# The norm of segment 2 transposed on TensorE, and a new order of the work

## The chip, the cores and the metric

The kernel runs on one core of one Trainium2 chip. The core has five engines that work side by side, each through its own queue in order: PE (matrix products; its weight loads are listed apart as PEld), DVE (vector), ACT (activation functions), POOL (general) and SP, which here only issues DMA transfers. Their results meet in two memories: SBUF, and PSUM with eight banks, into which PE writes. The metric is the time of one execution on the device in microseconds; the median of several runs counts.

## What is computed

The reference is one transformer block on 2048 tokens of 448 features. A conditioning vector gives six modulation vectors; the block is a modulated norm, an attention with a memory over four segments of 512 tokens, a second modulated norm, and a gated feed-forward part.

```python
mod = (silu(c) @ w_mod).reshape(1, 6, 1, -1)          # sa, ca, ga, sb, cb, gb
h = layernorm(x) * (1 + ca) + sa
x = x + ga * A(h)
h = layernorm(x) * (1 + cb) + sb
x = x + gb * B(h)

def A(x):                      # 16 heads of 28; 4 segments of 512
    q, k, v = split(x @ wq), split(x @ wk), split(x @ wv)
    M, z = 0, 0
    for s in range(4):
        a_dot = softmax(q[s] @ k[s].T * 28**-0.5 + causal_mask) @ v[s]
        a_mem = phi(q[s]) @ M / (phi(q[s]) @ z + 1e-6)
        o[s] = g * a_mem + (1 - g) * a_dot             # g = sigmoid(beta)
        M, z = M + phi(k[s]).T @ v[s], z + sum(phi(k[s]))
    return o @ wo

def B(x):
    return (sigmoid(x @ w_gate) * (x @ w_up)) @ w_down
```

Here phi(t) is t + 1 for positive t and exp(t) otherwise.

## The kernel before

**Stages.** Four segments of 512 tokens, each of four tiles of 128 tokens, pass through the same stages. `ln1` (from L618) normalizes x and brings it into the layout hT, features on partitions. `proj` (L655) makes q, k and v from it: 32 matmuls at L665 for q and k, 16 at L686 for v, with evictions out of PSUM by ACT (L673, L690). `attention` (L730) handles four heads at once, in four such groups (hc): logits at L746 into four adjacent PSUM banks, exp by ACT at L755, the causal mask by POOL at L761, the product with v at L769, and, after segment 0, the product with the memory at L783; DVE turns and scales the result (L776 to L817). `memory` (L703) applies phi to k, transposes it by DMA (pk<-pq, L708) and updates M (L714 to L727). `wo_ln2` (L821) applies the output weights (L831), adds the residual (L835) and makes the second norm. `ffn` (L843) makes 14 chunks of 128 hidden features: gate and up matmuls (L848, L856), tanh by ACT (L882), the gating product by DVE (L885), then the down product (L895), the residual (L901) and the output transfer (L903).

**The norm and its transposition.** `layer_norms` (L557) does statistics on DVE (L566, L567), the reciprocal root on POOL (L573, L574) and the scaling into an xn buffer on DVE (L582). There are six xn buffers. From there two ways lead to hT:

- For segments 0 and 1, `ln1` takes the branch at L622: PE transposes (L634, sixteen 128x128 products with the identity into four PSUM banks), and each bank is evicted with the modulation in the same instruction, two by ACT (L642) and two by DVE (L645).
- For segments 2 and 3, and for the second norm of all segments, SP issues four DMA transposes (`transposed`, L590; they appear as L592, hT<-xn), and four instructions modulate hT in place (`modulated`, L596): two on ACT (L602) and two on DVE (L605).

**The loads.** All weights come in once by DMA, nearly all issued by SP: q, k, v, x, the modulation weights (wm, at L347), the output weights (L505), then gate, up and down (L509 to L512). At most eight transfers are out at a time, and transposes go through the same queue. The output and down weights are multiplied by ga and gb in place (L544 on POOL; L551 on DVE for the first `wdd` of 14 chunks, on POOL for the rest).

**The order.** The order of instructions on every engine is worked out on the host before the program is built. Every piece of work is a node with an engine, a duration in ns, its dependencies, the buffers and banks it takes, and a priority. `Graph.run` (L110) plays the program through with these durations; whenever an engine is free, it takes the ready node with the highest sum of priority and remaining path. A load's duration is its size over a rate in bytes per ns (`load`, L327). The priorities are the numbers in `PRM` (L22), one per kind of work; `attention` is also held back by release times from `pace` (L914), and those of segment 0 get `a0` on top. `Graph.fill` (L187) puts dummy matmuls (L930, L933) into gaps of PE that the plan shows. On the chip each engine then follows its list in order, whatever the real durations are.

```python
    def pace(i):
        return PRM["T0"] + PRM["STEP0"] * min(i, NHC) + PRM["STEP"] * max(i - NHC, 0)
```

Of the kernel before, what the change touches and what calls it, by code (L numbers as in the profile page):

```python
# [11 lines left out]
ALU = mybir.AluOpType  # L12
# [8 lines left out]

PRM = dict(T0=6000, STEP0=500.0, STEP=10100.0, lg=77000, ex=-37000, mask=-11000, wo=58000, tanh=44500,  # L22
           up=77000, f=172500, dn=-486800, phi=-81000, t=-83000, ln1_1=-16000, ln1_2=-57000, ln1_3=-52000,
           mem=-12000, pj_0=44000, pj_1=-15000, pj_2=-94000, pj_3=9000, ot=339000, stall=300, wds=18000,
           wos=144000, wdd=4, mod=35000, a0=39000, w0=-37000, stay=120000)

# [181 lines left out]
def kernel(  # L208
# [16 lines left out]
    nc = tc.nc  # L225
# [118 lines left out]
    def load_wm(engs, j0, nj, flat, prio, deps=()):  # L344
        t = flat[0:CP, 0:NK * nj * D].rearrange("p (k n) -> p k n", k=NK)
        h = NK // len(engs)
        ns = [load(eng, t[:, i * h:(i + 1) * h, :], wm_cols[:, i * h:(i + 1) * h, j0 * D:(j0 + nj) * D],  # L347
                   CP * h * nj * D * 2, prio=prio, deps=deps, rate=240.0 if nj < 4 else 290.0)
              for i, eng in enumerate(engs)]
        for j in range(j0, j0 + nj):  # L350
            wm_at[j] = t[:, :, (j - j0) * D:(j - j0 + 1) * D]
            wml[j] = ns
# [97 lines left out]
    def mod_cols(j, vi, prio):  # L450
        b = bank()

        def mm():

            for kc, r0, r1 in ((0, 0, P), (1, 0, P), (2, 0, P), (3, 0, KR), (3, KR, P))[:4 if vi < 2 else 5]:
                for k in range(NK):
                    nc.tensor.matmul(pf(b)[r0:r1, kc:kc + 1], lhsT=wm_at[j][:, k, kc * P:kc * P + r1 - r0],
                                     rhs=silu[:, k:k + 1], start=(k == 0), stop=(k == NK - 1))
        n = add("PE", (16 if vi < 2 else 20) * 55, mm, [n_silu, *wml[j]], take=[b], prio=prio, mode="F")

# [21 lines left out]
    def padded(st, dst, loads, eng, prio):  # L482
        ns = []
        for k in range(NK):
            def fn(k=k, r=ROWS[k]):
# [3 lines left out]
                else:  # L489
# [15 lines left out]
    l_wo = [load("SP", wo_sb[h * HP:h * HP + Dh, :, :],  # L505
                 A_wo.rearrange("(c h e) n -> h e c n", h=4, e=Dh)[h], Dh * NHC * D * 2, [n_wopad], prio=lp - MEG * 4, rate=225.0)
            for h in range(4)]
# [49 lines left out]
    def layer_norms(srcs, deps, prio=0, hT=None, prev=None, twice=False):  # L557
# [13 lines left out]
        def rstd():  # L571
            r = rs_r[:, mv.at, 0:w]
            nc.gpsimd.tensor_scalar(r, mv_r[:, mv.at, 0:w, 1], EPS, None, op0=ALU.add)  # L573
            nc.gpsimd.tensor_tensor(r, r, mhalf[:, 0:w], ALU.pow)  # L574
        b = pool_op(860 if w == 1 else 1330, rstd, stats, prio, use=[mv])
        got = []
        for t, src in enumerate(srcs):
            xn = Slot("xn")

            def norm(t=t, src=src, xn=xn):  # L580
                for dst, x in ((xn_r[:, xn.at, 0:D], src), (xn_r[:, xn.at, D:NK * P], src[:, 3 * P:D]))[:1 + twice]:
                    nc.vector.tensor_scalar(dst, x, mv_r[:, mv.at, t, 0:1], rs_r[:, mv.at, t:t + 1],  # L582
                                            op0=ALU.subtract, op1=ALU.mult)
            n = dve(300 + 110 * twice, norm, [b, n_pads, prev], prio, take=[xn] if prev or not hT else [xn, hT],
                use=[mv], lock=0)
            prev = n
            got.append((n, xn))
# [30 lines left out]
    def ln1(s):  # L618
        hT = Slot("hT")
        out_ = []  # L620
        tiles = range(s * TPS, (s + 1) * TPS)
        if s < 2:  # L622
            top = BIG - 2 * MEG if s == 0 else PRM["ln1_1"]
            if s == 0:
# [69 lines left out]
    def phi(src, dst, deps, slots, take, prio):  # L694

        e = Slot("e")
        a = act(530, lambda: nc.scalar.activation(e_r[:, e.at, 0, :], src(), AF.Exp), deps, take=[e], use=slots, prio=prio)  # L697
        b = dve(210, lambda: nc.vector.tensor_scalar(e_r[:, e.at, 1, :], src(), 0.0, 1.0, op0=ALU.max, op1=ALU.add),
                [a], use=[e, *slots], prio=prio, lock=0)
# [30 lines left out]
    def attention(s, hc, oT, release, prev):  # L730
# [58 lines left out]
        def rec():  # L789
# [3 lines left out]
            nc.vector.tensor_tensor(r, r, coef[:, 0:w, hc, :], ALU.mult)  # L793
        r = dve(450 if w == 2 else 350, rec, [*parts, n_coef, n_opad], take=[R], use=[A], prio=PRM["t"] + a0, lock=320 if w == 2 else 230)

# [169 lines left out]
```

## Time and profile before

| what | value |
|---|---|
| median of 7 runs | 255.34 us (253.79 to 257.28) |
| the profiled execution | 255.64 us, of which the span is 253.6 us |
| mean granted TensorE clock | 0.991 of full speed |
| busy: PE, DVE, ACT, POOL | 241.5, 182.1, 157.3, 100.8 us |
| sum of all exp instructions (L755, 48) | 77.2 us on ACT |
| transposes by PE (L634, 32) | 2.3 us on PE, 219 ns each |
| evictions with modulation, ACT / DVE (L642 / L645) | 828 and 786 / 542 ns each |
| modulation in place, ACT / DVE (L602 / L605) | 829 and 820 / 516 ns each |
| DMA transposes hT<-xn (24), issue to landing | 2.4 us at least, 4.6 median, 10.9 at most |
| DMA transposes pk<-pq (12), issue to landing | 2.4 us at least, 2.4 median, 6.3 at most |

The span is the time from the first to the last instruction; the rest of an execution lies around it. An engine's busy time is the time in which at least one of its instructions runs. PE's matmuls are pipelined, so that neighbours overlap in the records: a 128x512 matmul is listed with 380 ns, and the next starts 216 ns after it. The page also cuts the span into 40 slices of 6.3 us, with a digit for the busy tenths of each:

```profile
PE   7999976889999999999999999999999999999994
DVE  7589935648977989999976999982487882453223
ACT  2589958989999969988915756866342232323110
PEclk9999997999999999999999999999999999999999
DMA  6999999321241010013401000210100022100002
GB/s 189 301 296 297 307 156 290 77 29 21 23 83 22 3 21 16 9 21 44 84 14 63 0 0 3 54 28 8 49 18 4 0 41 41 39 18 19 0 3 72
```

The input transfers fill the first 45 us (rows DMA and GB/s). PEclk is the TensorE clock that was granted, in tenths.

### The profile page before, as it was taken

To read this page: it belongs to the slowest core of one execution; us is meant where nothing else is said; L and a number is where in the kernel's file an instruction comes from. 1 tells how busy PE (TensorE), PEld (TensorE's weight loads), DVE (VectorE), ACT (ScalarE), POOL (GpSimd) and SP (SyncE) were. 2 spreads that over 40 slices of the span, in tenths; PEclk is the share of its full clock that TensorE was granted. 3 is DMA by queue.
4 is the path that set the end of the run, shared out by engine and by line. 5 is a ranking of instruction groups with operands and counts; after the bars stand their busy time and mean duration, and the time that the engine had idled before them with its cause. 6 is when DMAs were issued, how large, how long until landed. Compare 5 with 4: busy or idle time off the path is not lost.

```text
span 253.6 us, 4521 instructions
## 1 busy us (share of the span) xinstructions
PE 241.5 (95%) x1643; PEld 102.7 (40%) x1643; DVE 182.1 (72%) x411; ACT 157.3 (62%) x202; POOL 100.8 (40%) x164
## 2 busy tenths in 40 slices
PE   7999976889999999999999999999999999999994
PEld 2545432334434344444453433334333445334342
DVE  7589935648977989999976999982487882453223
ACT  2589958989999969988915756866342232323110
POOL 7745932224997544756350246632131220000000
PEclk9999997999999999999999999999999999999999
DMA  6999999321241010013401000210100022100002
GB/s 189 301 296 297 307 156 290 77 29 21 23 83 22 3 21 16 9 21 44 84 14 63 0 0 3 54 28 8 49 18 4 0 41 41 39 18 19 0 3 72
DMA packets 30142, 17.52 MB, mean 69 GB/s; under 512 B 20648, under 2 KB 28776, under 8 KB 30120
## 3 DMA queue, kind: packets, MB, share of 16 engines
q1 hardware_dynamic: 29592, 16.60, 28.5%
q10 hardware_dynamic: 528, 0.63, 0.9%
q8 instruction: 13, 0.21, 0.4%
q14 instruction: 9, 0.07, 0.1%
HBM read 10.67 MB, written 1.84 MB: 49 GB/s over the span
## 4 chain that ended last, share of the span: by engine, by line
PE 65%; DVE 12%; DMA 10%; ACT 6%; POOL 2%; issue 2%; SPq 1%; DVEq 0%; ACTq 0%
PE ps L848 28%; PE ps L895 15%; PE ps L665 5%; DMA pk<-pq 4%; PE ps L856 4%; PE ps L746 3%; DMA hT<-xn 3%; PE ps L831 3%; PE ps L769 3%; ACT pT L755 3%; DMA wd_sb<-in_A_wk_dram 2%; DVE fT L885 2%; PE ps L686 2%; DVE A L776 2%; POOL wo_sb L544 2%
## 5 line engine op out<-in xcount | busy, mean ns | idle before, releaser
L755 ACT ACTIVATE pT<-ps 128x2048 bf16<-128x2048 f32 (+1 forms) x48 | 77.2, 1608 | 16.8 <-PE ps L746 14.1
L761 POOL TENSOR_SCALAR_AFFINE_SELECT pT<-pT 128x512 bf16<-128x512 bf16 x64 | 44.1, 702 | 73.5 <-ACT pT L755 73.5
L882 ACT ACTIVATE tt<-ps 128x512 f32<-128x512 f32 x56 | 33.4, 603 | 51.9 <-PE ps L856 40.3
L885 DVE SCALAR_TENSOR_TENSOR fT<-tt,ps 128x512 bf16<-128x512 f32 x56 | 37.9, 682 | 26.7 <-ACT tt L882 22.7
L848 PE MATMUL ps<-hT,wu_sb 128*128 128x512 bf16 x182 | 48.5, 380 | 0.5 <-ACT pT L755 0.5
L848 PE MATMUL ps<-hT,wg_sb 128*128 128x512 bf16 x182 | 48.7, 381 | 0.0
L895 PE MATMUL ps<-wd_sb,fT 128*128 128x448 bf16 x224 | 45.7, 353 | 0.0
L895 PEld LDWEIGHTS <-fT 128*128 128x128 bf16 x224 | 21.4, 98 | 21.0 <-issue 0.8
L848 PEld LDWEIGHTS <-wu_sb 128*128 128x128 bf16 x182 | 16.9, 98 | 21.3 <-issue 1.8
L848 PEld LDWEIGHTS <-wg_sb 128*128 128x128 bf16 x182 | 15.5, 98 | 24.0 <-issue 9.7
L746 PE MATMUL ps<-qT,kT 28*128 28x512 bf16 (+3 forms) x256 | 17.6, 302 | 3.8 <-ACT pT L755 3.5
L566 DVE BATCH_NORM_STATS2 st<-x_sb 128x6 f32<-128x448 bf16 x32 | 19.5, 610 | 2.4 <-DMA x_sb<-in_A_x_dram 2.2
L776 DVE STREAM_TRANSPOSE A<-ps 128x512 f32<-128x512 f32 x28 | 19.1, 700 | 0.6 <-PE ps L783 0.5
L815 POOL TENSOR_TENSOR O<-U 128x448 bf16<-128x448 f32 x12 | 13.7, 1140 | 11.3 <-DVE U L813 11.3
L582 DVE TENSOR_SCALAR xn<-x_sb,mv,rs 128x448 bf16<-128x448 bf16 (+1 forms) x48 | 16.9, 408 | 0.8 <-POOL rs L574 0.8
L700 DVE TENSOR_TENSOR pq<-e 128x512 bf16<-128x512 bf16 x24 | 12.1, 506 | 7.3 <-ACT e L697 6.0
L665 PE MATMUL ps<-hT,wq_sb 128*128 128x512 bf16 x64 | 16.7, 380 | 0.1
L665 PE MATMUL ps<-hT,wk_sb 128*128 128x512 bf16 x64 | 16.5, 380 | 0.0
L574 POOL TENSOR_TENSOR rs<-rs,mhalf 128x1 f32<-128x1 f32 (+1 forms) x23 | 15.2, 663 | 1.9
L901 DVE TENSOR_TENSOR ot<-ps,x_sb 128x448 bf16<-128x448 f32 x16 | 9.8, 620 | 8.1 <-PE ps L895 7.3
L686 PE MATMUL ps<-wv_sb,hT 128*128 128x448 bf16 x64 | 15.3, 386 | 0.0
L813 DVE TENSOR_TENSOR U<-A,R 128x896 f32<-128x896 f32 x12 | 13.3, 1105 | 1.8 <-POOL O L815 1.6
(104 smaller groups left out, 285.8 us busy)
## 6 DMA issues: line engine op xcount, KB each, us to landing
out_dram<-ot SPq DMA_DIRECT2D x16, 112.0 KB, 1.7
fT<-in_w_mod_dram SPq DMA_DIRECT2D x1, 1568.0 KB, 11.7
x_sb<-in_A_x_dram SPq DMA_DIRECT2D x3, 448.0 KB, 5.4
wg_sb<-in_B_w_gate_dram SPq DMA_DIRECT2D x3, 448.0 KB, 7.6
wu_sb<-in_B_w_up_dram SPq DMA_DIRECT2D x3, 448.0 KB
wd_sb<-in_B_w_down_dram SPq DMA_DIRECT2D x2, 448.0 KB
wd_sb<-in_B_w_down_dram SPq DMA_DIRECT2D x2, 336.0 KB, 6.4
pT<-in_w_mod_dram ACTq DMA_DIRECT2D x1, 392.0 KB
```

The costliest lines, as they stand in the source:

```text
L566: nc.vector.bn_stats(st_r[:, st.at, :], src)
L582: nc.vector.tensor_scalar(dst, x, mv_r[:, mv.at, t, 0:1], rs_r[:, mv.at, t:t + 1], op0=ALU.subtract, op1=ALU.mult)
L665: nc.tensor.matmul(pf(b), lhsT=w_sb[:, kc, hc * 4:(hc + 1) * 4, :].rearrange("p h e -> p (h e)"), rhs=hT_r[:, hT.at, kc, :], start=(kc == ...
L686: nc.tensor.matmul(pf(b)[:, 0:D], lhsT=hT_r[:, hT.at, kc, t * P:(t + 1) * P], rhs=wv_sb[:, kc, :], start=(kc == 0), stop=(kc == NK - 1))
L746: nc.tensor.matmul(ps[:, lg.at + hs, o:o + nq], lhsT=kT_r[r, k.at, hc, kb * P:(kb + 1) * P], rhs=qT_r[r, q.at, hc, kb * P:L], start=True, ...
L755: nc.scalar.activation(pT_r[:, pT.at, :, w0:w0 + wid], ps[:, lg.at:lg.at + 4, 0:wid], AF.Exp, scale=scale)
L761: nc.gpsimd.affine_select(out=blk, in_=blk, compare_op=ALU.is_ge, fill=0.0, base=0, pattern=[[0, 4], [1, P]], channel_multiplier=-1)
L776: nc.vector.transpose(A_r[:, A.at, i, :, :].rearrange("p b e -> p (b e)"), pf(b))
L848: nc.tensor.matmul(pf(b), lhsT=w_sb[:, k, fc * P:(fc + 1) * P], rhs=hT_r[:, hT.at, k, :], start=(k == 0 and not late), stop=(k == n - 1 an ...
L882: a = act(500, lambda gp=gp, tt=tt: nc.scalar.activation(tt_r[:, tt.at, :], pf(gp), AF.Tanh, scale=0.5), [g], use=[gp, tt], prio=PRM["tanh"])
L885: fns.append(dve(605, lambda up=up, tt=tt, ft=ft: nc.vector.scalar_tensor_tensor(fT_r[:, ft.at, :], tt_r[:, tt.at, :], 1.0, pf(up), op0=AL ...
L895: nc.tensor.matmul(pf(b)[:, 0:D], lhsT=fT_r[:, fts[fc].at, t * P:(t + 1) * P], rhs=wd_sb[:, fc, :], start=(fc == 0), stop=(fc == NFC - 1))
```

## The change

Segment 2 takes the branch of segments 0 and 1: sixteen PE transposes and four evictions that modulate, in place of four DMA transposes and four modulations. Segment 3 and the second norms keep the DMA transposes.

The numbers that the planner works with change too: the rates of the modulation and output weight loads are lower, and some durations are set anew. All entries of `PRM` but a few have new values, so that the order on every engine is worked out again. The instructions are otherwise the same, but for two chunks of the down weights (`wdd` 4 to 6) that DVE scales instead of POOL.

```diff
-PRM = dict(T0=6000, STEP0=500.0, STEP=10100.0, lg=77000, ex=-37000, mask=-11000, wo=58000, tanh=44500,
-           up=77000, f=172500, dn=-486800, phi=-81000, t=-83000, ln1_1=-16000, ln1_2=-57000, ln1_3=-52000,
-           mem=-12000, pj_0=44000, pj_1=-15000, pj_2=-94000, pj_3=9000, ot=339000, stall=300, wds=18000,
-           wos=144000, wdd=4, mod=35000, a0=39000, w0=-37000, stay=120000)
+PRM = dict(T0=5000, STEP0=-1500.0, STEP=10000.0, lg=76000, ex=15000, mask=49000, wo=79000, tanh=-15500,
+           up=81000, f=175500, dn=-495800, phi=-82000, t=-80000, ln1_1=-17000, ln1_2=-57000, ln1_3=-52000,
+           mem=-32000, pj_0=36000, pj_1=5000, pj_2=-43000, pj_3=9000, ot=399000, stall=300, wds=-42000,
+           wos=144000, wdd=6, mod=-26000, a0=99000, w0=-36000, stay=120000)
...
-                   CP * h * nj * D * 2, prio=prio, deps=deps, rate=240.0 if nj < 4 else 290.0)
+                   CP * h * nj * D * 2, prio=prio, deps=deps, rate=190.0 if nj < 4 else 245.0)
...
-        n = add("PE", (16 if vi < 2 else 20) * 55, mm, [n_silu, *wml[j]], take=[b], prio=prio, mode="F")
+        n = add("PE", (16 if vi < 2 else 20) * 40, mm, [n_silu, *wml[j]], take=[b], prio=prio, mode="F")
...
-                 A_wo.rearrange("(c h e) n -> h e c n", h=4, e=Dh)[h], Dh * NHC * D * 2, [n_wopad], prio=lp - MEG * 4, rate=225.0)
+                 A_wo.rearrange("(c h e) n -> h e c n", h=4, e=Dh)[h], Dh * NHC * D * 2, [n_wopad], prio=lp - MEG * 4, rate=195.0)
...
-        b = pool_op(860 if w == 1 else 1330, rstd, stats, prio, use=[mv])
+        b = pool_op(860 if w == 1 else 1500, rstd, stats, prio, use=[mv])
...
-            n = dve(300 + 110 * twice, norm, [b, n_pads, prev], prio, take=[xn] if prev or not hT else [xn, hT],
+            n = dve(300 + 210 * twice, norm, [b, n_pads, prev], prio, take=[xn] if prev or not hT else [xn, hT],
...
-        if s < 2:
-            top = BIG - 2 * MEG if s == 0 else PRM["ln1_1"]
+        if s < 3:
+            top = BIG - 2 * MEG if s == 0 else PRM[f"ln1_{s}"]
...
-        b = dve(210, lambda: nc.vector.tensor_scalar(e_r[:, e.at, 1, :], src(), 0.0, 1.0, op0=ALU.max, op1=ALU.add),
+        b = dve(260, lambda: nc.vector.tensor_scalar(e_r[:, e.at, 1, :], src(), 0.0, 1.0, op0=ALU.max, op1=ALU.add),
...
-        r = dve(450 if w == 2 else 350, rec, [*parts, n_coef, n_opad], take=[R], use=[A], prio=PRM["t"] + a0, lock=320 if w == 2 else 230)
+        r = dve(520 if w == 2 else 430, rec, [*parts, n_coef, n_opad], take=[R], use=[A], prio=PRM["t"] + a0, lock=330 if w == 2 else 250)
```

## The prediction

> **What bounds the kernel now.** I read the engine rows first, then the stages, then the waits of the one bad stage, then its instructions in order of time.
>
> The windows view, cut at the places where the character of the work changes (columns: stretch, its length, then busy microseconds of PE, PEld, DVE, ACT, POOL with instruction counts, granted clock, DMA share, GB/s):
>
> ```profile
> 11.00:33.50 22.50, 22.36 (x186) 10.29 (x183) 18.92 (x55) 21.54 (x32) 15.93 (x27) 1.00 1.15 289
> 33.50:40.00 6.50, 3.09 (x29) 1.24 (x29) 2.96 (x8) 3.34 (x5) 0.70 (x1) 1.00 1.02 214
> 40.00:57.00 17.00, 14.81 (x121) 6.33 (x121) 8.35 (x23) 15.08 (x20) 5.03 (x8) 0.90 0.61 110
> 57.00:76.00 19.00, 18.41 (x142) 7.88 (x140) 16.41 (x39) 18.47 (x27) 14.65 (x22) 1.00 0.25 42
> 76.00:137.00 61.00, 60.98 (x454) 26.05 (x442) 54.73 (x116) 47.61 (x56) 31.94 (x43) 1.00 0.15 31
> 137.00:167.00 30.00, 28.97 (x204) 10.95 (x200) 26.97 (x60) 20.41 (x21) 13.64 (x22) 1.00 0.09 18
> 167.00:248.00 81.00, 81.00 (x449) 34.21 (x448) 42.84 (x81) 27.18 (x39) 10.38 (x17) 1.00 0.07 19
> ```
>
> From 76 us to the end PE has work at every moment (0.02 + 1.03 + 0.00 us idle in 172), so the end is the sum of PE's work plus whatever PE lost earlier. From 11 to 76 us the feed-forward stage has not begun and ACT is the full engine: 21.54 of 22.5, 15.08 of 17, 18.47 of 19. In between lies a hole, 33.5 to 40, in which every engine is half empty. The waits view of 33 to 57 us names it (us in total, times, longest):
>
> ```profile
> DVE hT L605 <- DMA hT<-xn: 4.3, 2, 3.4
> PE ps L746 <- ACT pT L755: 3.5, 2, 3.3
> ACT hT L602 <- DMA hT<-xn: 3.2, 1, 3.2
> PEld L714 <- DMA pk<-pq: 2.4, 2, 1.6
> ACT pT L755 <- PE ps L746: 1.9, 2, 1.2
> ```
>
> And the timeline of SP's queue, ACT, DVE and PE there (start, length, what; in brackets the idle time before it and who ended it):
>
> ```profile
> 24.61 10.03 SPq L592 DMA_TRANSPOSE hT<-xn  x4
> 34.69 0.59 SPq L329 DMA_DIRECT2D wu_sb<-in_B_w_up_dram  x1
> 35.38 2.15 SPq L329 DMA_DIRECT2D wd_sb<-in_B_w_down_dram  x4
> 37.63 1.76 SPq L708 DMA_TRANSPOSE pk<-pq  x1
> ...
> 37.39 0.81 ACT L602 ACTIVATE hT<-hT,cols 128x512 bf16<-128x512 bf16 x1 [3.16 <-DMA hT<-xn]
> 38.11 1.86 ACT L755 ACTIVATE pT<-ps 128x2048 bf16<-128x2048 f32 x1
> ...
> 37.43 0.74 DVE L605 TENSOR_SCALAR hT<-hT,cols 128x512 bf16<-128x512 bf16 x2 [3.41 <-DMA hT<-xn]
> ...
> 40.02 0.40 PE L746 MATMUL ps<-qT,kT 28*128 28x384 bf16 x8 [3.33 <-ACT pT L755]
> 40.35 4.13 PE L686 MATMUL ps<-wv_sb,hT 128*128 128x448 bf16 x12
> ```
>
> Segment 2's four transposes sit in SP's queue behind weight loads. SP needs 10.03 us to issue them; the last lands at 37.2. The modulation that waits for them heads ACT's and DVE's in-order queues, so an exp whose logits are long ready starts at 38.11 and the next logits only at 40.02. PE's 3.33 us of silence is then followed by a second loss: the window 40.9 to 44.3 has a granted clock of 0.50, and the 12 matmuls of L686 take 4.13 us where 12 x 189 ns (the spacing of the same matmuls elsewhere) is 2.27.
>
> **The change part by part.** All sums are against the profiled execution: 255.64 us (span 253.6 and 2.0 around it), 0.30 above the median of 255.34.
>
> *A. Four DMA transposes and four modulations of segment 2 go.* The stall they cause is 3.16 us on ACT, 3.41 on DVE, 3.33 on PE. ACT is the full engine around it, so I take ACT's: -3.2. What is late next is the same ACT queue with nothing to wait for; DVE and PE have slack behind it until 57 us.
> Here a rule speaks against the change. In this trace a transpose of this shape costs SP at least 1.19 us and lands 2.4 us after its issue when nothing is ahead of it (median 4.6, worst 10.9). The Trainium skill, "Advanced Engine Details and Errata", section X-Bar Transpose (TRN2), says that transposing DMAs are as fast as plain ones, 350 to 400 GB/s: an estimate from it is 4 x 131 KB / 350 = 1.5 us for the four, so their going would be worth 1.5 and the final sum -2.7. I follow the trace: what is removed is the wait for the last landing with the queue in it, not the transfer.
>
> *B. The half-speed clock after the hole goes with it.* PE loses 4.13 - 2.27 = 1.86 us; the part that ACT felt is the 1.24 us it waited for the late L746. Between 0 and -1.9; I take -1.2.
>
> *C. Sixteen PE transposes come in (L634).* The row for segment 1 is 16 in 1.28 us at 22.54, start to start 56 ns: 16 x 56 = 0.9 us. PE is full in that stage (22.36 of 22.5), so nothing covers it: +0.9. They add a wait, for the four xn of segment 2 from DVE, with projections and logits queued behind them on PE; the last of these xn ended at 25.7 us, and DVE had done their statistics by 19.5, so I charge the wait nothing; DVE's 3.6 idle of 22.5 us there is its cover. The Trainium skill, "TensorE: Matmul & The Clock Gate", Part 4: PE-mode transpose, puts one at about 275 ns in a kernel and says transposes do not count as activity for the clock: by it 16 x 275 = 4.4 us, and the sum would be -0.9. The trace has them overlapping at 219 ns each with the clock at 1.00 from 20 to 30 us; I take 0.9.
>
> *D. Four evictions out of PSUM replace the four modulations.* ACT: 2 x 0.81 us (L642) for 2 x 0.82 (L602), nothing. DVE: 2 x 0.54 (L645) for 2 x 0.41 (L605), +0.3, covered by DVE's idle time (8.65 of 17 us in 40 to 57); if that cover were gone it costs 0.3. Each of the four takes a PSUM bank for about a microsecond, while the logits need four adjacent ones. No row shows that conflict alone; below it is nothing, above it is the longest wait of an exp for logits (L755 on L746), 1.7. I take 0, since segment 1 did the same at 22.5 us and PE idled 0.06 us from 20 to 30.
>
> *E. SP's queue is shorter.* The last up-projection load and the four down-projection loads, issued at 34.69 to 37.5, move ahead by up to the 10.03 us of SP time; the pk transposes behind them landed 6.3 and 4.7 us after issue where 2.4 is normal. PE waited 0.61 and 1.15 us for pk at 45.6 and 52.9. Ends 0 and -1.8; I take the middle, -0.9. Segment 3's four DMA transposes stay, and may come earlier: three of its norms (L582) ran only at 38.08, since the six xn buffers were held until segment 2's transposes had landed.
>
> *F. Everything else is the order.* The planner gets slower load rates (the rates set when matmuls of wm and wo are placed), 40 for 55 ns a matmul of L457, and longer DVE and POOL durations; with them all priorities. What they say: attention of segment 0 is much more urgent (exp -37000 + 39000 becomes 15000 + 99000), heads are released from 5.0 us and the fifth at -1.0 instead of 8.0, one per 10.0 instead of 10.1 us; tanh falls below exp (44500 against -37000 becomes -15500 against 15000); the scaling of the down weights comes later, two more of it on DVE (2 x 0.60 us more there, 2 x 1.10 less on POOL). No row of this trace shows the new order. On the gain side, what is left of PE's losses from 11 to 248 us bounds it: 7.4 idle + 1.9 clock + about 2 of dummy matmuls (L933, 9 x 216 ns) = 11.3, less A, B and E, so -6 at most. On the loss side the nearest row is 137 to 167, where DVE is 90% full and PE loses 1.03 in 30 us; spread over 76 to 248 that is +6. I take 0.
>
> Sum: -3.2 - 1.2 + 0.9 - 0.9 = -4.4. 255.64 - 4.4 = 251.2, and 250.9 against the median.
>
> **The rivals.**
>
> *R1, the hole moves instead of closing.* Segment 3's transposes and the first pk transposes use the same queue and the same loads; the planner still reckons the feed-forward weights at 400 GB/s where the page shows about 300. If the new order puts segment 3's modulation early on ACT and DVE, they wait as segment 2's did. For it: the first of them, issued at 39.5, landed some 5 us later, and DVE waited 0.88 us at 47.6. Against: without segment 2's, the loads end some microseconds sooner. Half of A and B returns, +2.2, and E is nothing, +0.9: 254.0.
>
> *R2, slower: exp ahead of tanh starves PE of banks.* Before the change tanh's priority is above exp's. With exp first, each gate and up pair of banks waits up to one exp more (1.89 us), and the logits take four of the eight. Place: 76 to 167 us, beside the 18 exps of 128x2048 that run there. Against it: PE lost 0.02 us from 76 to 137, so there is some depth, and ACT is only 78% busy there. It decides from 0.39 us per exp, which turns the gain into a loss of 1% (18 x 0.39 = 7.0 = 4.4 + 2.6). At 0.45 it is +8.1: 259.0.
>
> *R3, the new order also packs the attention phase.* The dummies and waits of 57 to 76 (0.6 + 0.6) and part of 40 to 57 go: -3 more, 248.
>
> **How the numbers follow.** About 1% is what a measurement of this kernel can tell from no change: faster is below 252.8, slower above 257.9. Main case, 250.9 with its own range of 249 to 252.8: 0.42. R3: 0.16. R1 and all others that end between 252.8 and 257.9: 0.20. R2 and other losses from the order: 0.22. Faster 0.58, same 0.20, slower 0.22. The range 245.5 to 259 leaves out about 0.06 below (F's gain end, 251 - 6) and about 0.12 above.
>
> **What would show it.** A and B: no hT<-xn wait of ACT or DVE over 1 us before 45 us, no PE gap over 2 us, clock 1.00 from 20 to 60. C: 48 transposes at L634, still some 1.3 us for sixteen. E: 20 transposes hT<-xn, pk landing in under 4 us. R1: ACT or DVE waiting on hT<-xn or PE on pk for 2 us or more. R2: PE idle of several us from 76 to 167 released by ACT tt or DVE fT. The prediction fails if the first feed-forward matmul (76.1 us now) does not come 3 us or more sooner, or if it does and PE is no longer full behind it.

## The result and the profile after

| | before | after |
|---|---|---|
| median | 255.72 us (253.79 to 259.77, 33 runs) | 253.79 us (251.95 to 258.62, 14 runs) |
| ratio, 95% interval | 1 | 0.9914 (0.9885 to 0.9942) |
| profiled execution / its span | 255.64 / 253.6 us | 252.78 / 251.0 us |
| first projection matmul / first feed-forward matmul | 11.10 / 76.13 us | 11.99 / 73.30 us |
| ACT between these two: busy / idle | 58.46 / 6.57 us | 59.91 / 1.39 us |
| from the first feed-forward matmul to the end | 177.5 us | 177.7 us |

The kernel became 0.9% faster: 1.9 us by the medians and 2.2 us by the ratio, the right direction and half or less of the 4.4 us forecast. (The medians here are of all runs; the ratios, and the medians by clock further down, leave out runs over 1.5% above the fastest of their kernel.) The second half of the kernel did not move; all of the difference is in when the feed-forward stage begins. These are the lines for the stretch between the two matmuls, before and then after, in the columns of the windows view (ACT is the fourth busy time):

```profile
11.10:76.13 65.03, 58.70 (x475) 25.73 (x473) 46.72 (x123) 58.46 (x81) 36.34 (x58) 0.97 0.73 162
```

```profile
12.00:73.30 61.30, 58.14 (x498) 26.63 (x497) 49.05 (x125) 59.91 (x82) 39.92 (x61) 1.00 0.65 159
```

The windows view of the kernel after, cut as before (length, busy us of PE, PEld, DVE, ACT, POOL, granted clock, DMA share, GB/s):

```profile
11.00:33.50 22.50, 22.44 (x170) 10.21 (x168) 17.95 (x53) 21.41 (x32) 15.88 (x29) 1.00 1.06 293
33.50:40.00 6.50, 6.41 (x73) 3.12 (x72) 4.56 (x12) 6.50 (x10) 2.20 (x4) 1.00 1.20 271
40.00:57.00 17.00, 15.27 (x136) 7.19 (x132) 11.77 (x28) 16.71 (x25) 12.63 (x15) 1.00 0.34 56
57.00:73.30 16.30, 15.03 (x130) 6.52 (x130) 15.20 (x37) 16.30 (x21) 10.16 (x18) 1.00 0.23 46
73.30:137.00 63.70, 62.69 (x463) 26.20 (x461) 57.69 (x126) 52.24 (x61) 30.34 (x42) 1.00 0.13 23
137.00:167.00 30.00, 29.45 (x192) 11.98 (x190) 26.50 (x56) 15.77 (x18) 11.48 (x18) 1.00 0.13 33
167.00:246.00 79.00, 79.00 (x441) 33.67 (x440) 40.71 (x76) 24.96 (x36) 8.55 (x15) 1.00 0.07 19
```

The hole of 33.5 to 40 us is full: ACT 6.50 of 6.50, PE 6.41. The clock is 1.00 in every stretch. What is left shows in the waits view of 33 to 57 us and in the timelines of SP and PE:

```profile
DVE xn L582 <- DMA hT<-xn: 1.4, 1, 1.4
PEld L714 <- DMA pk<-pq: 1.1, 1, 1.1
```

```profile
26.38 5.55 SPq L329 DMA_DIRECT2D wd_sb<-in_B_w_down_dram  x4
32.03 4.43 SPq L708 DMA_TRANSPOSE pk<-pq  x1
36.56 2.75 SPq L592 DMA_TRANSPOSE hT<-xn  x2
```

```profile
40.99 0.40 PE L714 MATMUL ps<-vt,pk 128*128 128x128 bf16 x4 [0.91 <-DMA pk<-pq]
41.23 0.39 PE L634 MATMUL ps<-ident,xn 128*128 128x128 bf16 x4
42.11 0.83 PE L634 MATMUL ps<-ident,xn 128*128 128x128 bf16 x12 [0.49 <-DVE M_sb L721]
```

The down-projection loads now go out 9 us sooner, and right behind them stands the first pk transpose: SP needs 4.43 us for a single one. PE comes to the memory update (L714) before that has landed. Here it waits only 0.91 us. A second profile of the same kernel, taken in a later comparison (e15: 0.9912, 0.9881 to 0.9943), shows another size of it:

```profile
42.32 0.40 PE L714 MATMUL ps<-vt,pk 128*128 128x128 bf16 x4 [2.17 <-DMA pk<-pq]
42.56 0.39 PE L634 MATMUL ps<-ident,xn 128*128 128x128 bf16 x4
43.44 0.83 PE L634 MATMUL ps<-ident,xn 128*128 128x128 bf16 x12 [0.49 <-DVE M_sb L721]
44.22 1.60 PE L474 MATMUL ps<-fT,silu_bc 112*128 112x448 bf16 x4
45.75 0.61 PE L746 MATMUL ps<-qT,kT 28*128 28x512 bf16 x4
46.29 1.26 PE L769 MATMUL ps<-pT,vt 128*32 128x512 bf16 x16
```

PE stood 2.17 us, and then L474 takes 1.60 us where it took 0.92 in the first profile, L769 1.26 instead of 0.73: a stretch of half-speed clock is back (below: a window). The feed-forward starts at 76.04 and the span is 253.3 us, as before the change. Two profiles of one kernel show two sizes of this wait, so the sections below go by medians and by the mean granted clock that each run lists. One window of 3.4 us takes 1.7 us of 252, so 1.000 means none and about 0.993 means one; the mean does not say where in the run the window lies.

| mean clock of a run | before, 173 runs | after, 33 runs |
|---|---|---|
| 0.997 and over: no window | 2% (4 runs), median 256.0 us | 30%, median 252.3 us |
| 0.9885 to 0.997: one | 59%, median 255.7 us | 64%, median 254.2 us |
| below: more | 39%, median 256.7 us | 6% |

In the kernel after the runs without a window are some 2 us shorter than those with one. The four such runs of the kernel before are not shorter, so the mean clock alone does not tell a run's time.

### The profile page after: what moved, and what is told of

Same layout as the page of the kernel before. It is cut to its first block, busy times and chain, and to the rows that moved or that the text cites. A ratio compares the mean times of both kernels' runs of the same rounds, so it can differ in the third digit from the quotient of the medians.

```text
span 251.0 us, 4553 instructions
## 1 busy us (share of the span) xinstructions
PE 241.3 (96%) x1665; PEld 104.2 (41%) x1665; DVE 184.1 (73%) x413; ACT 157.2 (63%) x202; POOL 99.6 (40%) x162
## 4 chain that ended last, share of the span: by engine, by line
PE 56%; DVE 8%; ACT 4%; DMA 3%; issue 1%; DVEq 0%; ACTq 0%
PE ps L848 28%; PE ps L895 16%; PE ps L856 4%; DMA hT<-xn 2%; PE ps L831 2%; PE ps L746 2%; ACT pT L755 2%; PE ps L769 2%; DVE xn L582 1%; DVE fT L885 1%; DVE st L566 1%; DVE x_sb L835 1%; DVE A L776 1%; DVE ot L901 1%; PE ps L783 1%
## 5 line engine op out<-in xcount | busy, mean ns | idle before, releaser
L755 ACT ACTIVATE pT<-ps 128x2048 bf16<-128x2048 f32 (+1 forms) x48 | 77.4, 1613 | 17.7 <-PE ps L746 16.4
L895 PE MATMUL ps<-wd_sb,fT 128*128 128x448 bf16 x224 | 46.3, 353 | 0.5 <-DVE A L776 0.5
L848 PEld LDWEIGHTS <-wg_sb 128*128 128x128 bf16 x182 | 15.4, 97 | 23.8 <-issue 10.2
L582 DVE TENSOR_SCALAR xn<-x_sb,mv,rs 128x448 bf16<-128x448 bf16 (+1 forms) x48 | 16.7, 403 | 4.0 <-POOL rs L574 2.6
L746 PE MATMUL ps<-qT,kT 28*128 28x512 bf16 (+3 forms) x256 | 17.5, 302 | 1.8 <-ACT pT L755 1.3
L815 POOL TENSOR_TENSOR O<-U 128x448 bf16<-128x448 f32 x12 | 13.8, 1148 | 13.3 <-DVE U L813 13.3
L813 DVE TENSOR_TENSOR U<-A,R 128x896 f32<-128x896 f32 x12 | 13.4, 1113 | 0.2
L686 PE MATMUL ps<-wv_sb,hT 128*128 128x448 bf16 x64 | 13.5, 353 | 0.0
L746 PEld LDWEIGHTS <-kT 28*128 28x128 bf16 x256 | 5.5, 91 | 19.0 <-issue 18.3
```

The costliest lines, as they stand in the source:

```text
L746: nc.tensor.matmul(ps[:, lg.at + hs, o:o + nq], lhsT=kT_r[r, k.at, hc, kb * P:(kb + 1) * P], rhs=qT_r[r, q.at, hc, kb * P:L], start=True, ...
L755: nc.scalar.activation(pT_r[:, pT.at, :, w0:w0 + wid], ps[:, lg.at:lg.at + 4, 0:wid], AF.Exp, scale=scale)
L848: nc.tensor.matmul(pf(b), lhsT=w_sb[:, k, fc * P:(fc + 1) * P], rhs=hT_r[:, hT.at, k, :], start=(k == 0 and not late), stop=(k == n - 1 an ...
L895: nc.tensor.matmul(pf(b)[:, 0:D], lhsT=fT_r[:, fts[fc].at, t * P:(t + 1) * P], rhs=wd_sb[:, fc, :], start=(fc == 0), stop=(fc == NFC - 1))
```

## The experiments

Each kernel was compared with the kernel before on the same chip; ratios are to it, with 95% intervals. "Feed-forward" is the time of its first matmul in the profile. Unless a fixed order is named, the planner ran again and moved other work too.

**One half of the change, planned anew.** Three kernels ask whether the PE way or the new numbers bring the gain: the branch alone on the old numbers, the new numbers alone, and the change with one more norm (the second norm of segment 0) moved to PE.

```diff
 # e1_pe_only, in the kernel before
-        if s < 2:
-            top = BIG - 2 * MEG if s == 0 else PRM["ln1_1"]
+        if s < 3:
+            top = BIG - 2 * MEG if s == 0 else PRM[f"ln1_{s}"]
 # e2_order_only, in the kernel after
-        if s < 3:
+        if s < 2:
 # e4_ln2_pe, in the kernel after: wo_ln2, segment 0
-            trs.append(transposed(xn, ln, hT, t, PRM["wo"] + w0))
+            trs.append((ln, xn) if s == 0 else transposed(xn, ln, hT, t, PRM["wo"] + w0))
+        (for s == 0: the transposes and evictions of L622 to L645 with columns 2 and 3)
```

> The kernel before with only the branch for segment 2 changed; all planner numbers stay. If the four DMA transposes and the hole they cause are what the change gains (theory H), no wait on hT<-xn over 1 us is left before 40 us, the first feed-forward matmul comes at 72.5 to 73.5 us instead of 76.1, and the time is 0.985 to 0.992 of before. If the new numbers are needed to make use of the closed hole (theory O), the hole closes here too, but the first feed-forward matmul stays within 1 us of 76.1 and the time is 0.996 to 1.004.

> The kernel after with segment 2 back on the DMA transposes; all planner numbers are the new ones. Theory H: ACT or DVE wait 2 us or more for hT<-xn again, the first feed-forward matmul comes after 75.5 us and the time is 0.998 to 1.005 of before. Theory O: the new numbers place the waiting modulation later, so the wait is under 1 us, the first feed-forward matmul comes at 73 to 74.5 and the time is 0.990 to 0.994.

> The kernel after with the second norm of segment 0 also transposed on PE, its modulation in the eviction; segment 2 as in after. If the chain output product, second norm, DMA transposes, modulation sets the start of the feed-forward stage in after (theory C), that start moves from 73.3 to 70.5 to 71.5 us and the time falls by about 2 us to 0.982 to 0.986 of before. If ACT's work ahead of it sets the start (theory A), the start moves by under 1 us and the time is 0.990 to 0.996, PE having 0.9 us more to do.

All three are slower than the kernel before: 1.0186 (1.0140 to 1.0233), 1.0208 (1.0170 to 1.0246) and 1.0100 (1.0070 to 1.0129). The longest waits of e1 on PE and of e2 on DVE in 33 to 57 us:

```profile
PE ps L714 <- DMA pk<-pq: 3.8, 1, 3.8
```

```profile
DVE hT L605 <- DMA hT<-xn: 5.8, 2, 5.0
```

In e1 no hT wait is left, and PE waits longer for pk than it had stood still before. That is a first sign that the hole moves. But these kernels don't tell the two halves apart: with another structure a set of priorities gives another order, and here that cost 1 to 2%, more than the effect in question. In e2, for one, the feed-forward begins at 76.5 us, nearly as in the kernel before, and the 5 us are lost behind it. The comparison needs an order that is held fixed.

**One half of the change, in a fixed order.** First the new order with segment 2 back on DMA: every engine keeps its place in the list, the PE transposes fall out, and SP issues each transpose as soon as its norm is there. The kernel was run twice: as e6 (six runs, median 256.18 us, no interval) and as e12.

```diff
 # e6_dma_in_after and e12_dma_again, in the kernel after
+                if by_dma is not None:          # segment 2, behind each xn
+                    nc.sync.dma_start_transpose(hT_r[:, by_dma.at, :, t * P:(t + 1) * P], xn_r[:, xn.at, :])
...
-                    for t in range(TPS):
+                    for t in range(TPS if s < 2 else 0):
...
-                    src, dst = pb(b)[0:r, 0:L], hT_r[0:r, hT.at, kc, :]
+                    dst = hT_r[0:r, hT.at, kc, :]
+                    src = pb(b)[0:r, 0:L] if s < 2 else dst
```

> The kernel after in its own order, but segment 2 transposed by DMA, each of the four issued as soon as its xn is there, and modulated in place where after evicts; the 16 PE transposes are left out. The output is the same. What it costs is the price of the DMA way without a change of order. If the new order has no place left where these transposes are waited for in line, it is as fast as after or 0.9 us faster (0.988 to 0.991 of before). If their place in the queue delays the pk transposes behind them, PE's wait for the first pk grows from 0.9 to 3 us or more and the time is 0.996 to 1.003 of before.

> The same kernel as e6_dma_in_after, once more, for an interval: 256.2 us there, with single times from 251.2 to 259.5. If the DMA way costs what that median says, 0.998 to 1.003 of before again and a wait of PE for the first pk of 4 us; if most of those runs were disturbed, 0.985 to 0.992.

e12 gives 0.9994 (0.9962 to 1.0025): the new order by itself is worth nothing that can be seen, and in it the PE way is worth 0.8% (0.4 to 1.2% by the two intervals), 2.0 us. SP's and PE's timelines of e6 show how the DMA way costs its time there (lines of the added code shift the numbers: L585 is the transpose of segment 2, L712 and L718 are L708 and L714):

```profile
30.08 6.82 SPq L329 DMA_DIRECT2D wd_sb<-in_B_w_down_dram  x4
37.01 1.40 SPq L585 DMA_TRANSPOSE hT<-xn  x1
38.46 1.44 SPq L712 DMA_TRANSPOSE pk<-pq  x1
```

```profile
43.95 0.61 PE L718 MATMUL ps<-vt,pk 128*128 128x128 bf16 x4 [4.27 <-DMA pk<-pq]
44.35 1.70 PE L474 MATMUL ps<-fT,silu_bc 112*128 112x448 bf16 x4
```

The segment's transposes are no longer what is waited for. They push the loads and the pk transpose back on SP, and PE waits 4.27 us for pk; from 43.3 to 50.1 us the clock is at 0.50. In e12's profile that wait is 2.80 us, less than the 4 us expected of it.

Then the old order without the transposes: nothing stands in for them (segment 2 takes segment 1's hT, so that segments 2 and 3 of the output differ from the reference). It prices A, B and E together, without C.

```diff
 # e7_no_transposes, in the kernel before
+            if hT in skipped:
+                return
...
-                    nc.scalar.activation(v, v, AF.Identity, scale=cols[0:r, vi + 1, kc:kc + 1],
+                    nc.scalar.activation(v, u, AF.Identity, scale=cols[0:r, vi + 1, kc:kc + 1],
```

> The kernel before in its own order, with segment 2's four DMA transposes left out and nothing in their place; its modulation reads segment 1's hT, so the output of segments 2 and 3 is not the reference's. Durations are unchanged. This is the prediction's A, B and E together: 5.3 us by its sum, 0.979 of before, with the first feed-forward matmul at 70.8. If ACT's backlog limits it (in after ACT was idle only 1.4 us before the feed-forward stage), or if the first pk still waits for the loads, 2.5 to 3.5 us: 0.986 to 0.990, first feed-forward matmul at 72.6 to 73.6.

0.9887 (0.9850 to 0.9923), 2.9 us where the prediction summed 5.3. Timelines of its PE and ACT (L722, L754, L763 are L714, L746, L755):

```profile
41.42 0.40 PE L722 MATMUL ps<-vt,pk 128*128 128x128 bf16 x4 [1.65 <-DMA pk<-pq]
42.91 0.55 PE L722 MATMUL ps<-vt,pk 128*128 128x128 bf16 x4 [1.09 <-DMA pk<-pq]
43.25 1.70 PE L474 MATMUL ps<-fT,silu_bc 112*128 112x448 bf16 x4
```

```profile
45.60 1.88 ACT L763 ACTIVATE pT<-ps 128x2048 bf16<-128x2048 f32 x1 [3.00 <-PE ps L754]
```

With the transposes wholly gone, PE stands 2.7 us for pk within 3 us, L474 runs at half speed, and ACT waits 3.00 us for the logits behind it: nearly the 3.16 us that it had waited for hT, 8 us later and for another transfer.

Last, the mirror of e12, run at the end: the old order kept, and segment 2 by PE, placed by hand.

```diff
 # e18_pe_in_before, in the kernel before, behind G.fill (tr and ev shortened)
+    for n in (*dmas, *hs):              # segment 2: four transposes, four modulations
+        G.order.remove(n)
+    for i in (4, 7):                    # two banks, two halves of 512 in each
+        for kc in ((1, 0) if i == 4 else (3, 2)):
+            at = ps[:, i, :].bitcast(BF16)[:, kc % 2 * L:(kc % 2 + 1) * L]
...
+            put("PE", 29400, tr)        # four transposes into at
+            put("ACT" if kc in MOD_ACT[0] else "DVE", (29780, 30250, 31540, 30900)[(1, 0, 3, 2).index(kc)], ev)
```

> The kernel before with its own order on every engine kept, but segment 2 by the PE way: the four DMA transposes go, sixteen PE transposes stand on PE at the place where the plan has 29.4 us (behind the projections of segment 1 that end there, two banks with two halves each), and the four modulations read these banks at once. No new plan. Theory Q (what the run without the transposes showed: the hole moves to the first pk transposes): no hT<-xn wait of ACT or DVE before 45 us, PE waits 2 to 4 us for pk at 41 to 44 us, the first feed-forward matmul some 62.5 to 64 us behind the first projection, ratio 0.986 to 0.992, no better than the kernel after, so the new order as such brought nothing. Theory N (the new order carries a part of the gain): the PE way alone in the old order stays at 0.993 to 1.000. Theory P (the prediction's A, B and E in full): feed-forward 60.5 us behind the first projection, 0.978 to 0.984.

0.9930 (0.9893 to 0.9967). This misses theory Q's range by 0.001 and lies at the edge of theory N's; the interval takes in both. The PE way in the old order brings 1.8 us, in the new order 2.0: within these intervals the PE way is the change's gain in either order, and what the new order adds to it (0.9930 to 0.9914) is not told from nothing. Its profile is one without the pk wait, so that Q's 2 to 4 us of waiting did not show in it either:

```profile
30.20 1.06 PE L955 MATMUL ps<-ident,xn 128*128 128x128 bf16 x16
...
42.46 0.29 PE L752 MATMUL ps<-qT,kT 28*128 28x256 bf16 x4
42.68 0.78 PE L720 MATMUL ps<-vt,pk 128*128 128x128 bf16 x8
```

```profile
31.29 0.78 ACT L960 ACTIVATE hT<-ps,cols 128x512 bf16<-128x512 bf16 x1 [1.54 <-PE ps L955]
```

PE comes to the memory update at 42.68, when both pk have landed; the span is 250.8 us. In seven of its nine runs the mean clock was about 0.993, though, and in the two others 1.000. The medians of these groups are 254.4 and 252.8 us. The 1.54 us on ACT belong to the place chosen by hand.

**Single terms.** C doubled (the sixteen transposes of segment 2 made twice); B alone (fourteen dummy matmuls on PE ahead of the hole of the kernel before, so that the clock holds); and the later start of the kernel after undone (fewer dummies before 12 us).

```diff
 # e11_twice, in the kernel after
-                    for t in range(TPS):
+                    for t in (*range(TPS), *range(TPS)) if s == 2 else range(TPS):
 # e5_keep_clock, in the kernel before
+    v = next(n for n in G.order if n.eng == "PE" and 36000 < n.start < 36500)
+    G.order.insert(G.order.index(v), Node("PE", 0, lambda: dummy(v.take[0].at, 14, 36000), ...))
 # e3_fewer_dummies, in the kernel after
+            if a.end < 12000:
+                n = min(n, 6 if a.end < 8000 else 4)
```

> The kernel after with each of segment 2's 16 PE transposes done twice in place, the second overwriting the first with the same data; nothing else moves. This is the price of the prediction's term C alone. If PE's time before the feed-forward stage is on the path, the time rises by 0.9 us: 0.995 of before. If ACT or the transfers set that stage, the first feed-forward matmul stays within 0.3 us of 73.3 and the time at 0.991 to 0.992.

> The kernel before with 14 dummy matmuls (3.0 us) put on PE just ahead of the v product that precedes the hole; every other instruction keeps its order on its engine. PE then is silent for under 1 us before the next logits, so that the clock stays at 1.00 and the hole itself remains. If the slow clock costs what the prediction's term B says, the time falls by 1.2 us to 0.995 of before and the v products of L686 after the hole take 2.3 us instead of 4.13. If all of PE's 1.86 us were on the path, 0.993. If ACT hides it, 1.000.

> The kernel after with the two groups of dummy matmuls before 12 us cut from 8 and 6 to 6 and 4, as in the kernel before; every other instruction and its order are the same. If the longer dummies that the lower load rates bring delay the start (theory S), the first projection matmul comes at 11.1 to 11.5 us instead of 11.99, and the time is 0.4 to 0.9 us below that of after: 0.988 to 0.990 of before. If the loads set the start anyway, it stays at 11.9 or so and the time at 0.991.

e11: 0.9876 (0.9827 to 0.9926), not slower than the change itself; 0.9 us more would be 0.995, outside the interval, so C costs less than that. Its one profile is its longest run: PE waits 2.99 us for pk there and the feed-forward begins at 77.3, so the expected 73.3 is not tested by it.

e5: 0.9981 (0.9950 to 1.0013), which takes in both no gain and B's 1.2 us. The twelve matmuls of L686 behind the hole took 2.44 us instead of 4.13, but its profile has another dip at 47.8 us, around two waits for pk of 0.59 and 1.25 us, and one at the start, 10.2 to 13.6 us. Four of its fourteen runs had no window; their median is 254.3 us, where the one-window runs of the kernel before beside it took 255.4. That is near B's 1.2 us, but four runs do not settle it.

e3: 0.9879 (0.9823 to 0.9935); the first projection came at 11.06 instead of 11.99 and the feed-forward at 73.08 instead of 73.30, so that in the profile most of the earlier start was lost again; the weight load of L714 waits 1.7 us for pk there, where it waited 1.1.

**The new wait.** If pk lands late because loads are ahead of it, moving these loads must remove the wait. The four down-projection loads (wd) can stand later on SP, as long as the scalings that read them (L551) stand later too.

```diff
 # the move, in six kernels (T picks the place on SP; e8 picks it by count), behind G.fill
+    after = [n for n in G.order if n.eng == "SP" and n.start < T][-1]
+    for n in l_wd:
+        G.order.remove(n)
+    at = G.order.index(after) + 1
+    G.order[at:at] = l_wd
```

> The kernel after with the four down-weight loads moved on SP behind the first pk and the first two hT transposes; all other engines unchanged. If the loads ahead of it in the queue hold the first pk back (theory Q), it lands before 38 us, PE's wait of 0.9 us and DVE's of 1.4 us near 40 us are gone, and the time is 0.5 to 1 us below after: 0.987 to 0.989 of before. If the path runs through ACT alone, 0.990 to 0.992. If the down weights now come too late for their scaling on DVE at 44.5 us, DVE waits over 1 us there and the time is 0.994 or more.

> The kernel after with the four down-weight loads moved on SP behind all seven transposes that come before 45 us (three pk, four hT), and with the ten scalings of down weights that stood before 60 us moved to 79 to 106 us on POOL and DVE; nothing else moves. If the loads ahead of the transposes pin the start of the feed-forward stage (theory Q), the first pk lands at 35 us and the next two at 43 or before, PE no longer waits for pk near 40 us, and the first feed-forward matmul comes 0.5 to 1 us earlier than in after: 0.987 to 0.989 of before. If only ACT's own work sets it, 73.3 stays and the time is 0.991. If the later scalings on POOL hold up masks, POOL is late after 79 us and the time is above 0.994.

> The kernel after with the down-weight loads behind the early transposes, as in e9_wd_last, but with only the four scalings moved that would stand before their load has landed (three on POOL to 72 to 80 us, one on DVE to 80); the others stay at 52 us and later. If the 2 us that e9_wd_last lost after the start of the feed-forward stage came from its scalings on POOL and DVE, that stage is again 177.7 us long, starts at 72.5, and the time is 0.986 to 0.989 of before. If moving the loads itself costs there, 0.992 as in e9_wd_last.

> The kernel of e9_wd_last with the dummy matmuls before 12 us cut from 8 and 6 to 6 and 4 as well. Theory Q: the earlier start is no longer lost to the wait for pk, so that the first feed-forward matmul comes at 71.5 to 72.5 us and the time is 0.983 to 0.987 of before. If something else absorbs the start as in e3_fewer_dummies, it is as fast as e9_wd_last.

In the kernel after: behind the first pk and the first two hT transposes of segment 3 (e8), the first pk landed at 34.8 us instead of about 41, but the next two landed behind the loads, PE waited 3.5 us for them, and the ratio was 1.0047 (1.0024 to 1.0070). Behind all seven early transposes, with ten scalings moved (e9), no pk wait was left near 40 us and the feed-forward began at 72.45, 0.85 us sooner; but the stage after it took 179.7 us instead of 177.7: 0.9924 (0.9896 to 0.9952). With only four scalings moved (e13) it was 0.9912 (0.9885 to 0.9939); the feed-forward began 61.3 us behind the first projection, as in the kernel after, and took 178.7 us. With fewer start dummies as well (e10), 0.9944 (0.9917 to 0.9971), its first projection at 12.28 in a half-speed window from 11.1 to 14.5 us. In all eleven runs of e9 and fourteen of fifteen of e13 the mean clock was 0.997 or more: the half-speed window is gone. What that is worth is lost behind the feed-forward's start, and e9's profile shows one place:

```profile
93.10 1.91 DVE L813 TENSOR_TENSOR U<-A,R 128x896 f32<-128x896 f32 x1
```

```profile
95.66 1.02 PE L848 MATMUL ps<-hT,wg_sb 128*128 128x512 bf16 x4 [1.42 <-DVE fT L885]
```

From 90.72 to 94.06 us POOL runs a moved scaling (L551), a product (L815) and a second moved scaling, one behind the other. Beside them DVE's L700 and L813 take 1.24 and 1.91 us, where the same two in the kernel after, with no scaling near, take 0.43 and 1.08; the gating product comes late, and PE waits 1.42 us. e10's profile has the same (1.24, 1.91 and 1.41 us). That the moved scalings are the whole of the loss fits this but is not shown.

> The kernel of e7_no_transposes (the kernel before without segment 2's four transposes; output of segments 2 and 3 not the reference's) with the four down-weight loads behind the early pk and hT transposes on SP. If the pk held back by these loads keeps the rest of the gain (theory Q), PE waits under 0.5 us for pk before 45 us, the clock stays at 1.00, the first feed-forward matmul comes at 71 to 72 us and the time is 0.978 to 0.982 of before, which is the prediction's A, B and E. If ACT's own work keeps it, it is as fast as e7_no_transposes, 0.987 to 0.990.

> The kernel before, with segment 2 still by DMA, and only the four down-weight loads moved behind the early pk and hT transposes. The hole at 33.5 to 37 us stays, since segment 2's transposes were ahead of these loads already. Theory Q: pk lands within 3 us of its issue, PE's 1.8 us of waits for it go, and the time is 0.993 to 0.997. If the pk wait is hidden behind the slow clock and ACT, 0.998 to 1.001.

e14 is e7 with the loads behind the early transposes: 0.9885 (0.9859 to 0.9910), as e7. Its PE timeline says why:

```profile
40.02 0.82 PE L722 MATMUL ps<-vt,pk 128*128 128x128 bf16 x8
...
49.37 0.61 PE L722 MATMUL ps<-vt,pk 128*128 128x128 bf16 x4 [2.49 <-DMA pk<-pq]
```

The first two pk are on time, and the third waits behind the very loads that were moved: the hole has moved a second time. In the kernel before, with its hT hole left in place, moving the loads gives 0.9979 (0.9947 to 1.0011) (e16). PE no longer waits for pk in its profile, but PE's gap at the hT hole is 4.13 us instead of 3.33 there and the clock is at 0.50 for 6.8 us, so that e16 does not decide between its two expectations.

That left one kernel to settle it: e17, which is e18 with the loads behind all four pk of segment 0, in an order whose scalings come late enough anyway.

> The same, and the four down-projection loads stand on SP behind all four pk transposes of segment 0 (the scalings that need them come at 58 us and later in this order, so nothing new waits for them). Theory Q: what is left of the hole is the landing of pk behind loads, and with both gone ACT has nothing to wait for: no wait of PE for pk over 1 us before 57 us, clock 1.00 from 20 to 57, the feed-forward starts 60 to 61.5 us behind the first projection, ratio 0.976 to 0.985, better than both kernels. Rival W: the pk transposes still land late behind the gate and up loads, or another wait (ACT on the logits of PE) takes their place: feed-forward 62 to 64 us behind the first projection, 0.985 to 0.992, no better than e18.

0.9895 (0.9849 to 0.9942), 61.5 us from the first projection to the feed-forward: theory Q's time for the feed-forward is just missed, and so is its ratio (0.976 to 0.985); rival W's ratio came, though not its time. SP's timeline:

```profile
33.51 1.30 SPq L714 DMA_TRANSPOSE pk<-pq  x1
35.93 1.20 SPq L592 DMA_TRANSPOSE hT<-xn  x1
37.22 1.22 SPq L714 DMA_TRANSPOSE pk<-pq  x1
38.54 3.83 SPq L592 DMA_TRANSPOSE hT<-xn  x3
46.63 4.18 SPq L714 DMA_TRANSPOSE pk<-pq  x2
50.90 2.16 SPq L329 DMA_DIRECT2D wd_sb<-in_B_w_down_dram  x4
```

The first pk costs SP 1.30 us, where it cost 3.26 in e18 and 4.43 in the kernel after. No matmul waits for pk, and four of its six runs have the clock at 0.999 or more, where e18 had two of nine. Its profile takes as long for the stage as the clean profile of e18, 61.5 us, with ACT busy for 58.1: the waits left are 1.5 us of ACT at the hand-made place and 1.4 for casts of q and k (L679 on L671). This fits a pk wait that makes the difference from run to run, some 2 us, with ACT's own work behind it; six and nine runs, whose ratios do not differ beyond their intervals, do not show it. No kernel tried here beats the changed one by more than its interval.

The kernel after was run again beside e14 and e16:

> The kernel after, unchanged, on the chip of this call: 0.989 to 0.994 of before.

It gave the 0.9912 and the second profile shown in the result.

## Why the prediction was half right

**The bound (right).** PE loses 1.01, 0.55 and 0.00 us after 73.3 us; the stage from the feed-forward on lasts 177 to 178 us in both profiles of the kernel after, in the kernel before and in e6, e7 and e18. The end follows the feed-forward's start.

**A, B and E (the step that failed).** It is the sentence under A, "What is late next is the same ACT queue with nothing to wait for", and with it B taken in full and E as a gain. The prediction summed these to 5.3 us; with the transposes taken out of the old order and nothing put in (e7) they brought 2.9. The removed stall itself was sized correctly: in the profile with the short pk wait ACT's idle time falls from 6.57 to 1.39 us, by 5.2. But late next was PE's in-order queue at L714, which waits for the first pk transposes; these land at 41 to 44 us, unless loads are moved behind them. E had the transfers moving up, and they did (the first pk is issued at 32.03 instead of 37.63 us), but PE moved up too: it comes to L714 at 40.1 us instead of 44.6 and waits there. Some 64% of the runs of the kernel after still have one half-speed window. A run with one takes 254.2 us, without 252.3, so that the wait with its window is worth about 2 us. This takes the window to lie behind the pk wait, as it does in e15; the other runs have no profile.

Rival R1 had this as a possibility, though by another transfer: segment 3's modulation, its main suspect, made no engine wait 2 us, while DVE waited 1.4 and 2.6 us in the two profiles for xn buffers that segment 3's transposes held (L582), and it was pk, which R1 only named beside it, that kept PE waiting. That its 254.0 is nearly the median of 253.8 is in part luck, since it holds C's 0.9 us, which was not paid.

**C (wrong, small).** Charged 0.9 because PE looked full; doubled, it costs nothing that can be seen (e11). PE was full with work for ACT, the engine that sets this stage: while the transposes run, at 41.2 to 42.9 us in the kernel after, ACT has an exp and casts to do. The duration itself (about 56 ns from start to start, clock at 1.00) was right.

**D (right).** From 12 to 73 us of the first profile ACT waits 0.1 us ahead of an exp; the four evictions' banks cost nothing.

**F (right in sum, not in its parts).** The new order alone measures 0.9994. The zero was the middle between a gain and a loss of 6 us that no row told apart, so that it held is luck. In the profiled run the change holds two debts that the prediction did not see: the first projection is 0.89 us later, and ACT has 1.46 us more work ahead of the feed-forward. The phi groups on ACT in that stretch, before and then after (count | busy, mean ns | idle before):

```profile
L697 ACT ACTIVATE e<-kT 128x512 bf16<-128x512 bf16 x6 | 3.9, 654 | 0.0
L697 ACT ACTIVATE e<-qT 128x512 bf16<-128x512 bf16 x1 | 0.6, 645 | 0.0
```

```profile
L697 ACT ACTIVATE e<-kT 128x512 bf16<-128x512 bf16 x7 | 4.6, 690 | 0.0
L697 ACT ACTIVATE e<-qT 128x512 bf16<-128x512 bf16 x3 | 2.1, 711 | 0.0
```

Three more exps of phi lie ahead of the feed-forward (2.2 us more in these two rows), two modulations fewer, and the casts are each some 20 ns longer (L673 for k: 615 and 637 ns). So the run without a window balances: -5.18 + 1.46 + 0.89 = -2.83 us, the feed-forward's 76.13 to 73.30.

**R2 and R3 (did not come).** PE loses 1.56 us from 73 to 167 us where it lost 1.05, nothing like 18 waits for banks. Nor was the attention packed further: from 57 to 73 us ACT is 16.30 of 16.30 full, and PE fills 11 matmuls of dummies (L933).

**The stated test** asked for a feed-forward 3 us sooner. It came 2.83 us sooner in one profile and 0.09 in the other, so by its own test the forecast failed, and the two profiles together say how.

## What to carry to other kernels

When a wait on a queue goes, ask of every other transfer in that queue what stands ahead of it and who waits for it in order: a removed stall is worth its size only down to the next wait behind the same loads, here about half (2.9 of 5.3 us). Charge added work by the engine that sets the stage, not by the one that looks full beside it. And where a wait depends on when loads end, take two profiles and the granted clock of all runs before one profile's balance is believed; an order that was searched for one structure doesn't price another: here that cost 1 to 2%, twice.

## What the hardware showed beyond that

- The clock falls to 0.50 for 3.41 us or for twice that. It was 3.41 us behind gaps of PE of 3.33 us (the kernel before) and of 2.17 + 0.49 us (e15), and 6.83 us behind gaps of 4.27 us (e6) and of 2.80 us (e12). In each profile the changes lie whole multiples of 3.41 us apart: in e5 it falls at 10.21 and at 47.76 us, 11 x 3.413 later.
- No single length of silence separates the gaps that it follows from the others. Waits of 0.59 and 1.25 us with a few matmuls between them were followed by a fall (e5), and one gap of 2.49 us too (e14); a gap of 1.92 us was not (e1, at 123 us), nor was 0.91 + 0.49 us (the kernel after). The place of a gap on that raster of 3.41 us may be what decides; no run tests it.
- One DMA transpose holds SP for 1.2 to 1.8 us in most places, and the first pk behind four loads for 3.26 to 5.24 us (e18, e7, both profiles of the kernel after, e11). Behind these loads it lets PE go at 41 to 44 us; taken ahead of them it landed at 35 to 37 (e8, e9, e14, e17).
- With products and scalings on POOL beside it, a 128x896 product on DVE (L813) took 1.91 us in e9 and e10; its median there is 1.08 us.
- Fourteen dummy matmuls in a hole keep the clock there (2.44 for 4.13 us at L686). The time came back by 0.2%, with 0.5% inside the interval, so what the clock alone is worth at such a place stays open.
